# A decode kernel with a cached KV stream: loads alternate between K of the next job and V of the job in front of it

## The chip, the cores and the metric

The kernel runs on one core of one Trainium2 chip. The time is device microseconds (us). The kernel before took 631.83 us in the median of its first six runs (630.43 to 634.16). A profiled execution has a span (first to last instruction) a few microseconds shorter than the timed run; when a part of the span is quoted, it is from the profile.

## The reference, cut to what matters

The program runs two layers twice over a batch of eight single tokens: attention over a cached window, then an MLP, with the same weights and **the same caches** in both rounds.

```python
x = x + A(layernorm(x), k_cache, v_cache, wq, wo)   # round 0
x = x + B(layernorm(x), w1, b1, w2, b2)
x = x + A(layernorm(x), k_cache, v_cache, wq, wo)   # round 1, same caches
x = x + B(layernorm(x), w1, b1, w2, b2)
# A: W = 1024 cached positions, 32 heads of 128, 8 batch entries, bf16
#    p = softmax(q k^T / sqrt(128)); o = p v; out = o @ wo
# B: layernorm, w1, gelu, w2
```

K and V of one batch entry are 2 x 32 heads x 1024 x 128 in bf16. Each load brings two heads of K or V: a *unit* of 512 KB. The softmax is written without subtracting a maximum, so K of a group can be turned into scores as it comes.

## The kernel before

A *job* is one batch entry, one round, and eight head pairs (16 heads). A batch entry needs two jobs in round 0 and two in round 1. One of its two halves stays in SBUF between the rounds ("kept"); the other is loaded twice. So each batch entry costs 48 unit loads: 16 for each of two jobs of round 0 and 16 for the reloaded job of round 1. There are 24 unit buffers. A full kept half takes 16 of them, and 8 go round.

A small planner (class `Plan`) holds all tasks with their dependencies and assumed durations, plays them through in its own clock when the program is built, and emits the instructions of every engine in that order. On the chip each engine then runs its instructions strictly in order.

```python
NUNIT = 24                      # unit buffers of 512 KB
class Plan:
    HOP = 0.15
    LOAD_LATENCY = 1.9          # what the planner assumes for a load, plus 1.29 us of flow
    # ... emit(): an engine takes the ready task of lowest (rank, seq); loads go strictly in list order,
    #     each when the planner has a free "unit":
    #         landed = max(landed, now + self.LOAD_LATENCY) + t.flow; seen = landed + 0.4

def scores(job, z):             # z: group of four K units, 16 matmuls of N=512 on TensorE
    # ... needs all four K of the group, each transposed on VectorE first (turn)
    # afterwards the group's four buffers are free, unless the job is kept

def values(job, i):             # 16 matmuls per V unit; afterwards its buffer is free, unless kept

def add_loads(job):             # all K of a job, then all V
    job.loads = {}
    for which in "kv":
        for i in range(job.n):
            job.loads[which, i] = plan.add(SP, 0.07, lambda which=which, i=i: load(which, job, i),
                                           take="unit", flow=1.29)
            job.loads[which, i].pos = position[0]
            position[0] += 1

def chain(b, ...):              # batch entry b between the rounds, rank CHAIN = before everything else:
    # residual add, layernorm, w1, gelu, w2, layernorm, queries (160 matmuls), round_q, placed queries (qd2)
    # waits for the last job of round 0 of this entry

# order of the loads: l0[b] = the two jobs of round 0 (the second is kept), l1s[b] = the reloaded job of round 1
for job in l0[0]: add_loads(job)
# ... wo, w1, w2 (after load 32)
for job in l0[1]: add_loads(job)
for b in range(NB):
    if b < NB - 1: add_loads(l1s[b])
    if b + 2 < NB:
        for job in l0[b + 2]: add_loads(job)
add_loads(l1s[NB - 1])
```

The softmax here doesn't subtract the row's maximum and nothing guards it: scores larger than these inputs give would overflow.

## Time and profile before

| | |
|---|---|
| time, median of the first six runs | 631.83 us |
| span of the profiled run | 627.1 us |
| bytes moved, mean rate | 217.66 MB, 347 GB/s |
| steady period, residual add of one batch entry to the next (mean of six) | 70.4 us |
| the same if its 48 loads never stopped (48 x 1.28 us) | 61.5 us |

From the summary page of the kernel before: the span, the rate in 40 equal slices, and the packets.

```profile
span 627.1 us, 21695 instructions
...
GB/s 284 409 408 397 377 382 274 409 408 299 255 408 406 289 344 392 407 409 257 307 409 408 286 330 396 408 408 267 354 408 408 286 305 393 407 408 253 376 250 3
DMA packets 62720, 217.66 MB, mean 347 GB/s; under 512 B 6358, under 2 KB 12198, under 8 KB 61990
```

Undisturbed slices reach 406 to 409 GB/s. Between them lie slices at 255 to 299. The bytes alone take 217.66 MB / 409 GB/s = 532 us of the 627. The stream bounds the kernel, and what can be gained is in the slices where it falters.

One period from the timeline of VectorE (start, duration, line, operation, output<-inputs). The first and the third line are the residual adds that start the chains of two neighbouring entries; the second is the placement of the queries that ends the first chain.

```profile
...
279.74 0.13 DVE L531 TENSOR_TENSOR xT<-xT,att 128x5 f32<-128x5 f32 x1
...
301.39 0.81 DVE L351 TENSOR_TENSOR qd_151<-e_ps,mask_96 128x128 bf16<-128x128 f32 x4
...
351.65 0.12 DVE L531 TENSOR_TENSOR xT<-xT,att 128x5 f32<-128x5 f32 x1
```

The chain takes 301.39 - 279.74 = 21.7 us here, and the period 71.9 us. The windows of 3 us in that chain (columns: window, length, busy time and instruction count of each engine, granted clock, DMA share, GB/s):

```profile
...
core 0: us, PE busy (x) PEld busy (x) DVE busy (x) ACT busy (x) POOL busy (x), PEclk, DMA share, GB/s
...
282.00:285.00 3.00, 1.89 (x70) 1.89 (x70) 3.00 (x4) 0.00 (x0) 0.41 (x1) 0.50 0.71 281
285.00:288.00 3.00, 3.00 (x44) 1.12 (x42) 2.90 (x9) 0.22 (x1) 0.00 (x0) 0.50 0.04 12
288.00:291.00 3.00, 3.00 (x71) 1.76 (x68) 0.78 (x3) 0.00 (x0) 0.00 (x0) 0.50 0.73 217
...
300.00:303.00 3.00, 2.71 (x88) 2.71 (x88) 0.99 (x5) 0.18 (x1) 0.00 (x0) 0.50 0.18 60
303.00:306.00 3.00, 3.00 (x76) 1.97 (x77) 0.53 (x2) 0.00 (x0) 0.00 (x0) 0.50 0.90 304
```

The stream is dry twice, in 285-288 (12 GB/s) and in 300-303 (60 GB/s). The timeline of the queue that issues the loads (start, duration, instruction) tells why. Consecutive issues around the two holes:

```profile
...
276.06 0.54 SPq L364 DMA_DIRECT2D unit_124<-in_A_k_cache_dram  x1
287.51 0.54 SPq L364 DMA_DIRECT2D unit_118<-in_A_v_cache_dram  x1
...
293.29 0.54 SPq L364 DMA_DIRECT2D unit_124<-in_A_v_cache_dram  x1
301.72 0.54 SPq L364 DMA_DIRECT2D unit_118<-in_A_k_cache_dram  x1
```

From 276.06 to 287.51 nothing is issued: all eight circulating buffers hold K, and the first is freed only when four K have landed, been transposed and been scored. From 293.29 to 301.72 nothing is issued: eight V wait for their softmax and for the query matmuls. I call such gaps *issue holes*.

A measure used below: the *loss* of a stretch is its length minus its bytes / 409 GB/s. Over the second to the seventh chain of the kernel before the mean loss is 6.3 us inside the chain and 2.5 us between its end and the next chain.

### The profile page before, as it was taken

To read this page: it belongs to the slowest core of one execution; us is meant where nothing else is said; L and a number is where in the kernel's file an instruction comes from. 1 tells how busy PE (TensorE), PEld (TensorE's weight loads), DVE (VectorE), ACT (ScalarE), POOL (GpSimd) and SP (SyncE) were. 2 spreads that over 40 slices of the span, in tenths; PEclk is the share of its full clock that TensorE was granted. 3 is DMA by queue.
4 is the path that set the end of the run, shared out by engine and by line. 5 is a ranking of instruction groups with operands and counts; after the bars stand their busy time and mean duration, and the time that the engine had idled before them with its cause. 6 is when DMAs were issued, how large, how long until landed. Compare 5 with 4: busy or idle time off the path is not lost.

```text
span 627.1 us, 21695 instructions
## 1 busy us (share of the span) xinstructions
PE 438.7 (70%) x10016; PEld 307.6 (49%) x10016; DVE 308.0 (49%) x587; ACT 39.1 (6%) x115; POOL 13.9 (2%) x27
## 2 busy tenths in 40 slices
PE   1556319777777788668686788668777777668784
PEld 1333316555454564456363564456463564455474
DVE  2444044655536726645447726645546726545522
ACT  0000000000000001000000001000000001000000
POOL 2000000000000000000000000000000000000001
PEclk9999999999965556555655556555655556555655
DMA  7999997998799799997899799997999789997960
GB/s 284 409 408 397 377 382 274 409 408 299 255 408 406 289 344 392 407 409 257 307 409 408 286 330 396 408 408 267 354 408 408 286 305 393 407 408 253 376 250 3
DMA packets 62720, 217.66 MB, mean 347 GB/s; under 512 B 6358, under 2 KB 12198, under 8 KB 61990
## 3 DMA queue, kind: packets, MB, share of 16 engines
q1 hardware_dynamic: 62630, 216.29, 89.6%
q8 instruction: 78, 1.28, 0.8%
q14 instruction: 12, 0.10, 0.0%
HBM read 216.25 MB, written 0.01 MB: 345 GB/s over the span
## 4 chain that ended last, share of the span: by engine, by line
DMA 48%; PE 27%; issue 10%; DVE 8%; SPq 5%; POOL 0%; POOLq 0%; ACT 0%; DVEq 0%; ACTq 0%
DMA unit_127<-in_A_k_cache_dram 8%; DMA unit_119<-in_A_k_cache_dram 7%; PE s_ps L385 7%; PE o_ps L430 5%; PE q_ps L542 5%; DMA unit_118<-in_A_k_cache_dram 5%; DMA unit_119<-in_A_v_cache_dram 5%; DMA unit_127<-in_A_v_cache_dram 3%; PE o_ps L326 3%; PE h_ps L297 3%; DMA unit_137<-in_A_v_cache_dram 2%; DMA unit_131<-in_A_v_cache_dram 2%; DMA unit_135<-in_A_k_cache_dram 2%; DMA unit_136<-in_A_v_cache_dram 2%; DMA unit_133<-in_A_k_cache_dram 2%
## 5 line engine op out<-in xcount | busy, mean ns | idle before, releaser
L385 PEld LDWEIGHTS <-qd_150 128*16 128x16 bf16 x512 | 17.6, 103 | 82.7 <-issue 56.1
L454 PE MATMUL att<-ot,wo_sb 128*128 128x1 bf16 x1280 | 37.0, 165 | 24.2 <-DVE ot L445 12.2
L454 PEld LDWEIGHTS <-wo_sb 128*128 128x128 bf16 x1280 | 36.9, 104 | 25.4 <-issue 13.5
L542 PE MATMUL q_ps<-xn,wq_sb 128*128 128x1 bf16 x1280 | 35.8, 165 | 5.3 <-issue 5.3
L542 PEld LDWEIGHTS <-wq_sb 128*128 128x128 bf16 x1280 | 35.0, 104 | 7.3 <-issue 5.5
L297 PE MATMUL h_ps<-yT,w_sb 128*128 128x1 bf16 (+1 forms) x630 | 18.2, 166 | 28.8 <-DVE yT L265 26.0
L396 ACT ACTIVATE p_s<-s_ps 128x512 bf16<-128x512 f32 x32 | 19.1, 597 | 286.0 <-PE s_ps L385 286.0
L409 PE MATMUL sh_ps<-p_s,ident 128*32 128x64 bf16 x512 | 13.3, 238 | 33.6 <-DVE p_s L399 33.3
L399 DVE STREAM_TRANSPOSE p_s<-p_s 128x512 bf16<-128x512 bf16 x32 | 22.3, 697 | 26.8 <-ACT p_s L396 26.8
L422 DVE RECIPROCAL rd<-d_ps 128x16 f32<-128x16 f32 x32 | 7.9, 247 | 49.8 <-PE d_ps L418 49.8
L297 PEld LDWEIGHTS <-w_sb 128*128 128x128 bf16 x630 | 17.5, 104 | 29.6 <-DVE yT L265 15.7
L409 PEld LDWEIGHTS <-ident 128*32 128x32 bf16 x512 | 9.5, 117 | 41.9 <-DVE p_s L399 21.4
L385 PEld LDWEIGHTS <-qd_151 128*16 128x16 bf16 x512 | 13.8, 113 | 29.8 <-issue 26.6
L370 DVE STREAM_TRANSPOSE unit_118<-unit_118 128x1024 uint32<-128x1024 uint32 x12 | 14.9, 1242 | 23.4 <-DMA unit_118<-in_A_k_cache_dram 23.4
L260 POOL TENSOR_TENSOR ln_w<-ln_w,nhalf 128x1 f32<-128x1 f32 (+1 forms) x18 | 12.0, 665 | 602.2 <-DVE ln_w L257 598.1
L326 PEld LDWEIGHTS <-w_sb 128*128 128x128 bf16 x630 | 17.6, 104 | 12.0 <-issue 4.1
L351 DVE TENSOR_TENSOR qd_150<-e_ps,mask_96 128x128 bf16<-128x128 f32 x32 | 7.1, 282 | 29.7 <-PE e_ps L347 29.7
L370 DVE STREAM_TRANSPOSE unit_133<-unit_133 128x1024 uint32<-128x1024 uint32 x10 | 12.4, 1239 | 18.3 <-DMA unit_133<-in_A_k_cache_dram 18.3
L445 DVE TENSOR_TENSOR ot<-o_ps,rd 128x16 bf16<-128x16 f32 x16 | 2.5, 159 | 37.6 <-PE o_ps L430 37.6
L376 PE MATMUL s_ps<-ident,mask_l 2*128 2x512 bf16 x32 | 18.7, 586 | 0.0
L445 DVE TENSOR_TENSOR ot_149<-o_ps,rd 128x16 bf16<-128x16 f32 x16 | 3.6, 226 | 29.5 <-PE o_ps L430 29.5
L385 PE MATMUL s_ps<-unit_135,qd_150 128*16 128x512 bf16 x32 | 13.7, 566 | 5.8 <-DVE unit_135 L370 5.8
(304 smaller groups left out, 1158.3 us busy)
## 6 DMA issues: line engine op xcount, KB each, us to landing
unit_118<-in_A_k_cache_dram SPq DMA_DIRECT2D x12, 512.0 KB
unit_119<-in_A_k_cache_dram SPq DMA_DIRECT2D x12, 512.0 KB, 10.1
unit_120<-in_A_k_cache_dram SPq DMA_DIRECT2D x12, 512.0 KB
unit_121<-in_A_k_cache_dram SPq DMA_DIRECT2D x12, 512.0 KB, 15.1
unit_134<-in_A_k_cache_dram SPq DMA_DIRECT2D x11, 512.0 KB
unit_135<-in_A_k_cache_dram SPq DMA_DIRECT2D x11, 512.0 KB
unit_127<-in_A_k_cache_dram SPq DMA_DIRECT2D x11, 512.0 KB, 10.2
wq_sb<-in_A_wq_dram SPq DMA_DIRECT2D x5, 1024.0 KB, 6.8
```

The costliest lines, as they stand in the source:

```text
L260: nc.gpsimd.tensor_tensor(out=t["wv"][:], in0=t["wv"][:], in1=nhalf[:, 0:nb], op=ALU.pow)
L297: nc.tensor.matmul(t["h"][:, fc, :], lhsT=w1_sb[:, kc, fc * P:(fc + 1) * P], rhs=t["y"][:, kc, :], start=(kc == 0), stop=(kc == NKC - 1))
L326: nc.tensor.matmul(t["o"][:, n, :], lhsT=w2_sb[:, fc, n * P:(n + 1) * P], rhs=t["g"][:, fc, :], start=(fc == 0), stop=(fc == NFC - 1))
L370: nc.vector.transpose(t, t)
L376: nc.tensor.matmul(job.s_ps[:].rearrange("p (x u) -> p x u", u=2), lhsT=mask_l[:].rearrange("k x u i -> k (x u i)"), rhs=ident[0:2, None, ...
L385: nc.tensor.matmul(s_ps[32 * a:32 * a + 16, :].rearrange("p (t c) -> p t c", c=32), lhsT=qd[:, je, o:o + 16], rhs=k[:, je // 2, je % 2], s ...
L396: nc.scalar.activation(job.p_s[:], job.s_ps[:], ACT.Exp, scale=QSCALE, accum_out=job.rs[:])
L399: nc.vector.transpose(job.p_s[:], job.p_s[:])
L409: nc.tensor.matmul(job.sh_ps[32 * i:32 * i + 32, a], lhsT=ident[:, 32 * a:32 * a + 32], rhs=turned[:, :, 0:4, i], start=True, stop=True)
L430: nc.tensor.matmul(job.o_ps[:, 2 * i:2 * i + 2], lhsT=v[:, c * DH:(c + 1) * DH], rhs=job.p_v[:, a, c, 2 * z:2 * z + 2], start=(first and c ...
L454: nc.tensor.matmul(att[job.b][:, n:n + 1], lhsT=wo_sb[:, h, n * P:(n + 1) * P], rhs=job.ot[:, hi:hi + 1], start=(h == 0 and n == 0), stop= ...
L542: nc.tensor.matmul(t["q"][:, h:h + 1], lhsT=wq_sb[:, kc, h * DH:(h + 1) * DH], rhs=t["x"][:, kc, :], start=(kc == 0), stop=(kc == NKC - 1))
```

## The change

The intent: V of a job and K of the next job need different engines and different waiting. If they alternate, a V arrives when its probabilities have long been ready, so its buffer comes back at once; and VectorE, which needs 1.25 us for each K, sees a K only every 2.56 us.

```diff
+WP = (9, 16, 22, 26)
...
-    def add_loads(job):
-        job.loads = {}
-        for which in "kv":
-            for i in range(job.n):
-                job.loads[which, i] = plan.add(...)
+    def add_loads(jobs, extra):
+        for prev, job in zip([None] + jobs, jobs + [None]):
+            ks = [("k", job, i) for i in range(job.n)] if job else []
+            vs = [("v", prev, i) for i in range(prev.n)] if prev else []
+            while ks or vs:
+                for x in (ks, vs):
+                    if x:
+                        for f in extra.get(position[0], ()):
+                            f()
+                        add_load(*x.pop(0))
...
-    for job in l0[0]:
-        add_loads(job)
-    wo_ready = [...]
-    w_ready = [...]
-    # ... (the rest as shown above)
+    jobs = l0[0] + l0[1]
+    for b in range(NB):
+        jobs += [l1s[b]] + (l0[b + 2] if b + 2 < NB else [])
+    add_loads(jobs, {WP[0]: [first half of wo], WP[1]: [second half of wo], WP[2]: [w1], WP[3]: [w2]})
```

(The last lines are shortened: each entry of the dictionary adds one weight load ahead of the load with that number.)

Three things change at once: the *alternation*; a *shift*, since V of a job now comes with or after K of the next, so that the V that closes a batch entry lands eight loads later in the list; and the *weights*, which go in among the first 26 loads. The bytes, the 10016 matmuls and the 587 VectorE instructions stay.

More of the change, by code (lines that the diff above doesn't have):

```diff
@@ L48, in __init__ @@
         self.b, self.layer, self.p0, self.n, self.kept = b, layer, p0, n, kept
-        self.k, self.v = {}, {}
+        self.k, self.v, self.loads = {}, {}, {}
         self.o_ps = None
@@ L469, in _kernel, with add_load @@
     position = [0]
-    def add_loads(job):
-        job.loads = {}
-        for which in "kv":
-            for i in range(job.n):
-                job.loads[which, i] = plan.add(SP, 0.07, lambda which=which, i=i: load(which, job, i),
-                                               take="unit", flow=1.29)
-                job.loads[which, i].pos = position[0]
-                position[0] += 1
+    def add_load(which, job, i):
+        job.loads[which, i] = plan.add(SP, 0.07, lambda: load(which, job, i), take="unit", flow=1.29)
+        job.loads[which, i].pos = position[0]
+        position[0] += 1
+    def add_loads(jobs, extra):
[8 more added lines that the diff above has]
+                        add_load(*x.pop(0))
     def add_weights(us, fn):
@@ L588, in add_queries @@
         return expand(step, lambda: q1T[:, b, :], qd1)
-    for job in l0[0]:
-        add_loads(job)
-    wo_ready = [add_weights(7.0, lambda: load_wo(0, 16)), add_weights(7.0, lambda: load_wo(16, 32))]
-    w_ready = [add_weights(5.6, load_w1), add_weights(5.6, load_w2)]
-    for job in l0[1]:
-        add_loads(job)
-    for b in range(NB):
-        if b < NB - 1:
-            add_loads(l1s[b])
-        if b + 2 < NB:
-            for job in l0[b + 2]:
-                add_loads(job)
-    add_loads(l1s[NB - 1])
+    jobs = l0[0] + l0[1]
+    for b in range(NB):
+        jobs += [l1s[b]] + (l0[b + 2] if b + 2 < NB else [])
+    wo_ready, w_ready = [], []
+    add_loads(jobs, {
+        WP[0]: [lambda: wo_ready.append(add_weights(7.0, lambda: load_wo(0, 16)))],
+        WP[1]: [lambda: wo_ready.append(add_weights(7.0, lambda: load_wo(16, 32)))],
+        WP[2]: [lambda: w_ready.append(add_weights(5.6, load_w1))],
+        WP[3]: [lambda: w_ready.append(add_weights(5.6, load_w2))],
+    })
     qd = add_queries(0, [])
```

## The prediction

> **What bounds the kernel now.** The cache stream. The summary shows 217.66 MB at a mean of 347 GB/s, while undisturbed 3 us slices of the window table reach 401 to 416. (The Trainium skill, "DMA: Bandwidth & Descriptors", Specifications, gives a fabric ceiling of 435 GB/s; this trace never passes 416.) At 409 GB/s the bytes need 532 us of the 627 us span. A 512 KB unit lands every 1.28 us (issue spacing, 309-340 us). A steady period (one batch, 48 units) takes about 70 us against 48 x 1.28 = 61.5, so each of six loses about 8.5 us. At the end the stream stops at about 605 us and 21.6 us of work follow.
>
> **Where the loss sits.** While a batch's serial chain (layernorm, MLP, queries: 22.5 us from residual add to placed queries, 279.7 to 302.2) runs, 16 of 24 buffers hold kept K and V, so 8 circulate. The timeline of the DMA-issuing queue shows no issue from 276.1 to 287.5 (all eight hold K; scores wait for four landings, VectorE transposes of 1.25 us and 2.0 us of MLP matmuls) and none from 293.8 to 301.7 (eight V wait for softmax, 4.4 us of query matmuls and a 2.2 us pause). The window table shows 12 GB/s in 285-288 and 60 in 300-303.
>
> **What the change does.** No byte, matmul or vector instruction is added or removed; load order changes, every engine's order with it, and weights move into the first 26 loads. During a chain a V now arrives with its probabilities ready, so its buffer returns after about 0.5 us, and K arrives every 2.56 us, so transposes no longer crowd the chain. From the new instruction order I walk one steady chain by hand with the durations above. The first hole almost vanishes (estimate 0.5 us): four K are scored between the MLP products and five V are consumed before the queries. The second remains: the second K group is scored after the queries, leaving the queue empty for 3 to 5 us, plus a slow restart (a load issued into an empty queue at 301.7 landed 4.0 us later). Loss per period: about 5 us (estimate) for 8.5. Six periods gain about 21 us.
>
> **What it costs.** The V that closes a batch lands eight loads (10 us) later, so every chain starts later. That hurts at both ends: in the first chain the arriving K are kept, in the last they need queries not yet made; the eight buffers fill up and the stream should be nearly dry for 12 to 14 us in each (estimate), against about 6 us before. In the last chain part is offset: 24 loads follow its start, 32 before. Estimated starts: second chain 154 us (before 140), eighth 552 (before 562.7), then about 61 us to the end (before 64.5).
>
> **Predicted.** 615 us (-2.7%), range 602 to 629. Faster by over 2%: 0.60; within 2%: 0.34; slower: 0.06.
>
> **What would show it.** Issue holes of about 11 and 8 us per period become one of 6 to 8 us around the query matmuls; periods about 66 us; DMA share in 200-550 us up from 0.91-0.95 to about 0.96; a nearly dry stretch of over 10 us in the first chain (110-125 us) and in the last; PE and VectorE busy time unchanged within 2%.
>
> **What would make it wrong.** If K groups, now gathered over 10 us instead of 5, hold buffers so long that the stream stalls outside the chain, the gain vanishes. If V values queue behind the chain on PE, holes stay at 8 us. If the first and last chains overlap better than my walk says, it is below 602.

## The result and the profile after

| | before | after |
|---|---|---|
| median | 631.53 us (20 runs) | 651.36 us (10 runs) |
| ratio, 95% interval | | 1.031, 1.0285 to 1.0334 |
| span | 627.1 us | 649.1 us |
| second chain starts (1) | 140.3 us | 157.4 us |
| mean of the six periods from there | 70.4 us | 71.8 us |
| eighth chain starts | 562.7 us | 588.3 us |
| from there to the end | 64.4 us | 60.8 us |
| mean chain, second to seventh | 21.0 us | 25.6 us |

(1) Read from the residual adds on VectorE, as in the timeline above.

A ratio is the mean time of one kernel's fast runs over that of the other's of the same rounds, so it is not quite the ratio of the medians.

The change made the kernel 3.1% slower. The 22 us of span are: 17.1 before the second chain, 8.5 in the six periods, and -3.6 at the end. The shift moves eight loads (8 x 1.28 = 10.2 us) from behind the last chain to in front of the second, so as time lost the account reads: 6.9 us before the second chain, 8.5 in the periods, 6.6 at the end.

The same lines of the summary page, after:

```profile
span 649.1 us, 21675 instructions
...
GB/s 288 398 388 400 378 408 316 166 391 375 321 306 407 398 306 285 404 408 350 308 313 407 376 326 311 409 407 320 277 385 406 363 341 238 410 408 316 150 246 3
DMA packets 62720, 217.66 MB, mean 335 GB/s; under 512 B 6358, under 2 KB 12198, under 8 KB 61990
```

The bytes and the packets are the same to the digit. The mean rate is 335 GB/s instead of 347; low slices (166, 150) stand near both ends. The third chain on VectorE, with the start of the next. The second and the third line make the inputs of the first MLP matmuls (yT) and of the query matmuls (xn):

```profile
...
229.25 0.17 DVE L539 TENSOR_TENSOR xT<-xT,att 128x5 f32<-128x5 f32 x1 [0.59 <-PE att L455]
...
232.79 0.24 DVE L266 TENSOR_SCALAR yT<-xT,ln_mv,ln_w 128x5 bf16<-128x5 f32 x1
...
245.44 0.25 DVE L266 TENSOR_SCALAR xn<-xT,ln_mv,ln_w 128x5 bf16<-128x5 f32 x1
...
254.90 0.85 DVE L352 TENSOR_TENSOR qd_151<-e_ps,mask_96 128x128 bf16<-128x128 f32 x4
...
300.55 0.17 DVE L539 TENSOR_TENSOR xT<-xT,att 128x5 f32<-128x5 f32 x1 [0.59 <-PE att L455]
```

This chain takes 254.90 - 229.25 = 25.7 us, where the one shown of before took 21.7. Windows of 3 us in it (columns as before):

```profile
...
228.00:231.00 3.00, 3.00 (x76) 2.89 (x74) 2.18 (x6) 0.37 (x1) 0.00 (x0) 0.50 0.91 300
231.00:234.00 3.00, 0.95 (x36) 0.87 (x34) 1.96 (x7) 0.00 (x0) 0.54 (x1) 0.50 0.96 285
...
237.00:240.00 3.00, 2.65 (x55) 1.40 (x48) 1.50 (x4) 0.22 (x1) 0.00 (x0) 0.50 0.70 264
240.00:243.00 3.00, 2.87 (x79) 2.78 (x77) 1.47 (x3) 0.00 (x0) 0.00 (x0) 0.50 1.04 333
...
246.00:249.00 3.00, 2.42 (x90) 2.42 (x91) 1.17 (x1) 0.00 (x0) 0.00 (x0) 0.50 1.03 419
...
252.00:255.00 3.00, 2.55 (x33) 0.93 (x25) 1.27 (x2) 0.69 (x2) 0.00 (x0) 0.50 0.21 38
255.00:258.00 3.00, 2.79 (x44) 1.20 (x48) 1.61 (x7) 0.37 (x1) 0.00 (x0) 0.50 0.94 317
```

There is no window as dry as 285-288 was, but there are more low ones: of the fourteen windows from 222 to 264 us, one stands at 38 GB/s and eight at 264 to 333 (not all shown). Note 231-234: the DMA engines are busy for 0.96 of the window and move 285 GB/s. By the issues and the landings that the trace tells, about four or five loads are under way there. The same number are under way in 246-249, at 419 GB/s, so the number alone does not explain the low rate; the low windows lie in a hole or just behind one. The queue that issues:

```profile
...
219.96 0.55 SPq L365 DMA_DIRECT2D unit_134<-in_A_v_cache_dram  x1
227.01 0.54 SPq L365 DMA_DIRECT2D unit_128<-in_A_k_cache_dram  x1
...
234.45 0.53 SPq L365 DMA_DIRECT2D unit_125<-in_A_k_cache_dram  x1
238.66 0.54 SPq L365 DMA_DIRECT2D unit_130<-in_A_v_cache_dram  x1
...
243.44 0.54 SPq L365 DMA_DIRECT2D unit_130<-in_A_v_cache_dram  x1
247.20 0.54 SPq L365 DMA_DIRECT2D unit_128<-in_A_k_cache_dram  x1
253.27 0.54 SPq L365 DMA_DIRECT2D unit_136<-in_A_v_cache_dram  x1
```

The two holes have become four: 7.0 us before the chain starts, then 4.2 (234.45 to 238.66), 3.8 (243.44 to 247.20) and 6.1 us (247.20 to 253.27). They add up to 21 us, where the two holes before added up to 17 us in three of five chains (20 in the one shown). Now the chain of waits through this stretch (start, length, what; each piece was released by the one above it):

```profile
...
214.20 10.35 DMA unit_126<-in_A_v_cache_dram
...
224.59 0.59 PE o_ps L431 x16
225.18 1.92 PE s_ps L386 x12
227.10 0.45 SPq L365
...
227.65 6.13 DMA unit_125<-in_A_v_cache_dram
...
233.83 0.59 PE o_ps L431 x16
234.42 1.87 PE h_ps L298 x70
...
239.93 6.61 DMA unit_128<-in_A_v_cache_dram
```

A V that lands at 224.54 (issued at 214.20, one of the last behind a deep queue) is followed on TensorE by the second score group of the *next* job, and only that group, at 227.1, frees buffers. The reason lies in the load list: the V that alternate with these K belong to the half that is kept, so that using them frees nothing; the eight circulating buffers hold the four K of that group and four later loads that cannot be used before it. Its last K, issued at 212.22, landed at 223.26. The V issued at 227.65, after the hole, needs 6.13 us to land. TensorE waits for it, and the first MLP matmuls stand behind it. The same happens again from 239.93 to 246.58, in front of the query matmuls. TensorE's own records of these two waits (last bracket: idle time and what ended it):

```profile
...
233.83 0.59 PE L431 MATMUL o_ps<-p_v,unit_125 128*128 128x2 bf16 x16 [2.04 <-DMA unit_125<-in_A_v_cache_dram]
...
246.58 0.59 PE L431 MATMUL o_ps<-p_v,unit_128 128*128 128x2 bf16 x16 [3.17 <-DMA unit_128<-in_A_v_cache_dram]
...
253.19 0.29 PE L348 MATMUL e_ps<-qT,sel 128*128 128x32 bf16 x4
```

TensorE is idle for 5.2 us here. Not all of it is lost to the chain: yT was ready at 233.03 and xn at 245.69, so the matmuls behind the two V started about 1.3 us late each. The last line shows a third delay without any idle time: e_ps, which spreads the finished queries, stood behind a score group of four K and started 1.5 us after its input (qT, ready at 251.66). This delay of 1.5 us occurs in each of the six chains; the waits for V come to 3.8 us a chain in TensorE's idle time and to about 1.5 us in delay of the two matmul groups (means of the second to seventh chain). The chain grew by 4.6 us in the mean. The kernel before has no wait for V inside a chain.

The first chain is the other place. Its windows after:

```profile
...
111.00:114.00 3.00, 2.24 (x85) 2.27 (x85) 1.02 (x3) 0.00 (x0) 0.00 (x0) 1.00 0.19 74
...
120.00:123.00 3.00, 3.00 (x102) 2.70 (x99) 1.50 (x3) 0.19 (x1) 0.00 (x0) 1.00 0.02 5
123.00:126.00 3.00, 2.06 (x17) 0.47 (x16) 0.63 (x4) 0.00 (x0) 0.00 (x0) 1.00 0.56 175
```

From 111 to 126 us the rate is 5 to 212 GB/s. Here the K that arrive are kept K, which free nothing, so the eight circulating buffers fill up.

### The profile page after: what moved, and what is told of

It reads as the page before. It is cut to its first block, busy times and chain, and to the rows that moved or that the text cites. A ratio compares the mean times of both kernels' runs of the same rounds, so it can differ in the third digit from the quotient of the medians.

```text
span 649.1 us, 21675 instructions
## 1 busy us (share of the span) xinstructions
PE 421.8 (65%) x10016; PEld 305.1 (47%) x10016; DVE 313.9 (48%) x587; ACT 39.1 (6%) x115; POOL 14.0 (2%) x27
## 3 DMA queue, kind: packets, MB, share of 16 engines
q8 instruction: 78, 1.28, 0.8%
## 4 chain that ended last, share of the span: by engine, by line
DMA 71%; PE 16%; issue 7%; SPq 3%; DVE 2%; POOL 0%; POOLq 0%; ACT 0%; DVEq 0%
PE s_ps L386 6%; DMA unit_141<-in_A_v_cache_dram 5%; DMA unit_125<-in_A_v_cache_dram 4%; DMA unit_127<-in_A_v_cache_dram 4%; PE q_ps L550 3%; DMA unit_139<-in_A_v_cache_dram 3%; DMA unit_124<-in_A_v_cache_dram 3%; DMA unit_134<-in_A_v_cache_dram 3%; DMA unit_140<-in_A_v_cache_dram 3%; DMA unit_126<-in_A_v_cache_dram 3%; DMA unit_120<-in_A_v_cache_dram 3%; DMA unit_118<-in_A_v_cache_dram 3%; DMA unit_138<-in_A_v_cache_dram 3%; DMA unit_128<-in_A_v_cache_dram 3%; DMA unit_132<-in_A_v_cache_dram 3%
## 5 line engine op out<-in xcount | busy, mean ns | idle before, releaser
L386 PEld LDWEIGHTS <-qd_150 128*16 128x16 bf16 x512 | 13.7, 108 | 37.6 <-issue 36.9
L386 PEld LDWEIGHTS <-qd_151 128*16 128x16 bf16 x512 | 13.6, 111 | 26.6 <-issue 18.2
L371 DVE STREAM_TRANSPOSE unit_130<-unit_130 128x1024 uint32<-128x1024 uint32 x15 | 18.7, 1246 | 9.3 <-DMA unit_130<-in_A_k_cache_dram 9.3
L377 PE MATMUL s_ps<-ident,mask_l 2*128 2x512 bf16 x32 | 19.3, 604 | 0.0
L371 DVE STREAM_TRANSPOSE unit_120<-unit_120 128x1024 uint32<-128x1024 uint32 x9 | 11.2, 1241 | 15.7 <-DMA unit_120<-in_A_k_cache_dram 15.7
L371 DVE STREAM_TRANSPOSE unit_118<-unit_118 128x1024 uint32<-128x1024 uint32 x10 | 12.4, 1244 | 12.9 <-DMA unit_118<-in_A_k_cache_dram 12.9
L386 PE MATMUL s_ps<-unit_118,qd_150 128*16 128x512 bf16 x36 | 17.2, 617 | 1.9 <-DVE unit_118 L371 1.6
L415 ACT CAST p_v<-sh_ps 128x256 bf16<-128x256 f32 x32 | 11.9, 373 | 105.0 <-PE sh_ps L410 105.0
L431 PE MATMUL o_ps<-p_v,unit_141 128*128 128x2 bf16 x192 | 7.1, 166 | 16.6 <-DMA unit_141<-in_A_v_cache_dram 15.4
L371 DVE STREAM_TRANSPOSE unit_129<-unit_129 128x1024 uint32<-128x1024 uint32 x8 | 9.9, 1238 | 16.4 <-DMA unit_129<-in_A_k_cache_dram 16.4
L371 DVE STREAM_TRANSPOSE unit_140<-unit_140 128x1024 uint32<-128x1024 uint32 x8 | 10.0, 1245 | 16.2 <-DMA unit_140<-in_A_k_cache_dram 16.2
L386 PE MATMUL s_ps<-unit_130,qd_151 128*16 128x512 bf16 x36 | 16.9, 620 | 0.0
```

Source lines behind the costliest of these rows:

```text
L371: nc.vector.transpose(t, t)
L377: nc.tensor.matmul(job.s_ps[:].rearrange("p (x u) -> p x u", u=2), lhsT=mask_l[:].rearrange("k x u i -> k (x u i)"), rhs=ident[0:2, None, ...
L386: nc.tensor.matmul(s_ps[32 * a:32 * a + 16, :].rearrange("p (t c) -> p t c", c=32), lhsT=qd[:, je, o:o + 16], rhs=k[:, je // 2, je % 2], s ...
L415: nc.scalar.copy(job.p_v[:], job.sh_ps[:])
L431: nc.tensor.matmul(job.o_ps[:, 2 * i:2 * i + 2], lhsT=v[:, c * DH:(c + 1) * DH], rhs=job.p_v[:, a, c, 2 * z:2 * z + 2], start=(first and c ...
```

## The experiments

Theories:

- **ORDER**: TensorE runs in a fixed order, planned with a load latency of 1.9 us; V stand ahead of the chain's matmuls and have not landed.
- **GATHER**: a group of four K now takes eight loads to come together and holds buffers all the while.
- **SHIFT**, later made precise as **ENDS**: what costs is that the closing V and the chain come eight loads later, and that this is paid in the first and the last chain.
- **BUFFERS**: with eight circulating buffers, no order of loads can keep the queue filled through a chain.

Medians and ratios are against the kernel before in the same rounds (3 rounds each; its medians were 630.2 to 631.3 us). The granted clock differs between executions but does not follow the time: executions of the changed kernel at 0.66 and at 0.93 took 650.0 and 651.9 us. "Period" is the mean from the second chain's start; where the shift is taken back before the end, the shortened last period is left out.

| run | median us | ratio | second chain starts | period us | last chain to end |
|---|---|---|---|---|---|
| after_blk8 | 646.27 | 1.0236 | 162.5 | 69.3 | 64.3 |
| after_blk4 | 651.91 | 1.0331 | 159.4 | 71.5 | 62.5 |
| after_lat4 | 642.10 | 1.0169 | 156.4 | 70.4 | 59.1 |
| after_lat6 | 641.70 | 1.0178 | 155.9 | 71.2 | 57.2 |
| after_wp32 | 648.51 | 1.0281 | 157.2 | 70.8 | 61.4 |
| after_lastfix | 640.51 | 1.0165 | 157.7 | 71.0 | 64.7 |
| before_wpearly | 633.64 | 1.0050 | 144.2 | 70.4 | 64.8 |
| before_lat4 | 630.68 | 0.9984 | 139.8 | 70.7 | 65.6 |
| mid_blk1 | 634.43 | 1.0054 | 149.4 | 71.2 | 65.0 |
| mid_blk1_lat4 | 629.68 | 0.9986 | 149.4 | 70.4 | 64.6 |
| mid_blk8 | 625.95 | 0.9902 | 150.1 | 70.2 | 65.6 |
| mid_blk8_lat4 | 623.65 | 0.9883 | 150.1 | 69.9 | 64.2 |
| before_half24 | 635.93 | 1.0087 | 146.2 | 71.0 | 65.4 |
| before_half26 | 619.40 | 0.9812 | 146.1 | 68.2 | 62.6 |
| after_half26 | 619.88 | 0.9827 | 160.8 | 66.6 | 56.7 |
| mid_blk1_lat4_half26 | 607.03 | 0.9620 | 152.8 | 66.5 | 62.3 |

All are correct except the four "half" runs, which are wrong.

### after_blk8: the shift without the alternation

```diff
                 for x in (ks, vs):
-                    if x:
+                    for _ in range(min(8, len(x))):
```

> The changed kernel, but the loads go in blocks: eight K of the next job, then eight V of the job in front (the shift and the early weights stay, the alternation goes). Theory GATHER (a group of four K now takes eight loads to come together and holds buffers meanwhile): the steady period goes back to 70.4 us or less and only the later start remains, so about 641 us. Theory SHIFT (what costs is that the closing V and with it the chain come eight loads later; alternation is neutral): stays at 651 +- 3 us with periods near 71.8. Theory ORDER (PE runs values in a fixed order inside the chain and waits for V that have not landed): the chain, 25.3 us in the changed kernel, shortens to about 20-22 us because no V stands between the chain's first matmuls, about 640-645 us.

Measured: 646.27 us; periods 69.3 us, chains 22.5 us, second chain at 162.5 us. Without the alternation the periods are 1.1 us *shorter* than before, and all of the loss, more than all of it, lies at the ends. So the shift in itself does not lengthen a period. It does cost at the ends: 162.5 - 140.3 - 10.2 = 12.0 us before the second chain, and 64.3 - 64.4 + 10.2 = 10.1 us at the end.

### after_blk4: the same in fours

```diff
-                    if x:
+                    for _ in range(min(4, len(x))):
```

> The changed kernel with blocks of four K, four V. GATHER: a K group gathers in four loads, as in the kernel before, so nearly all of the loss per period comes back: periods 70.4 us or less, about 640 us. SHIFT: 651 +- 3 us. ORDER: V still stand inside the chain, in fours; chain 23-25 us, 645-651 us.

Measured: 651.91 us, periods 71.5 us. Here a K group gathers in four loads, just as before, and nothing comes back. GATHER, as the cause of the longer period by itself, is refuted. (The chains were 21.9 us, shorter than I expected under ORDER, and the period did not follow. So the length of the chain is not the whole story either.)

### after_lat4 and after_lat6: a planner that expects loads later

```diff
-    LOAD_LATENCY = 1.9
+    LOAD_LATENCY = 4.0      # 6.0 in after_lat6
```

> The changed kernel; only the planner's assumed latency of a load goes from 1.9 to 4.0 us (the trace shows 4 to 6.6 us from issue to landing after a hole), so it places fewer values ahead of the chain's matmuls. ORDER: waits of PE for V inside the chain (2.0 and 3.2 us in the third chain) go, the chain shortens from 25.3 to about 21 us, periods to 69 or less, total about 635 us. GATHER and SHIFT: the chain may shorten, but the period does not follow; 648-652 us.

> Dose: planner's latency 6.0 us. ORDER: waits for V inside the chains (3.8 us a chain in the changed kernel, 1.5 us at 4.0) fall to under 1 us, chain about 20 us, total as at 4.0 or slightly less: 638-643 us. If the gain at 4.0 was an accident of one order: anywhere, for instance back at 650.

Measured: 642.10 and 641.70 us, both about 9 us better than the change as it was. The waits of TensorE for V inside the chains (mean of the second to seventh) went from 3.8 us to 1.5 us at 4.0 and to nothing at 6.0, and the chains from 25.6 to 21.0 and 19.6 us. The third chain of after_lat6 on VectorE:

```profile
...
226.62 0.17 DVE L539 TENSOR_TENSOR xT<-xT,att 128x5 f32<-128x5 f32 x1 [0.59 <-PE att L455]
...
245.45 0.88 DVE L352 TENSOR_TENSOR qd<-e_ps,mask 128x128 bf16<-128x128 f32 x4 [3.94 <-PE e_ps L348]
...
```

It takes 18.8 us, where the changed kernel took 25.7. ORDER is right about the waits. What is worth 9 us is the edit, and the edit plans TensorE's whole order anew: at 6.0 the score group ahead of e_ps is gone too (e_ps starts within 0.1 us of its input in all six chains). So the runs show that the fixed order cost 9 us, not that the waits for V alone did. ORDER is wrong about the size: I had expected 635, and at 6.0, with no wait left, there is no further gain. The periods are 70.4 and 71.2 us, no shorter than in the kernel before.

### before_lat4: the control for it

```diff
-    LOAD_LATENCY = 1.9
+    LOAD_LATENCY = 4.0      # in the kernel before
```

> Control: the kernel before with the planner's latency at 4.0 us instead of 1.9. If the 9 us that the same edit brought to the changed kernel came from V standing ahead of the chain (ORDER), little happens here, where no V stands inside the chain: 628-634 us. If the planner's latency was simply wrong for any order, this gains some 9 us too: about 622 us.

Measured: 630.68 us, ratio 0.9984 with an interval from 0.9954 to 1.0014. The old order has no V inside the chain and gains nothing from the edit. The 9 us belong to the new order of loads.

### before_wpearly and after_wp32: the weights alone

In the kernel before, the weights go to loads 9, 16, 22 and 26 and the order of K and V stays; in the changed kernel, they go back behind load 32.

```diff
-        WP[0]: [...], WP[1]: [...], WP[2]: [...], WP[3]: [...],
+        32: [all four],
```

> The kernel before with one part of the change alone: the weights at loads 9, 16, 22 and 26 instead of after load 32. All theories: the same bytes precede the second chain, so within 1% of the kernel before (625-638 us); if the early weights were the cause of the 17 us by which the second chain starts later, this would be about 640 us or more.

> The changed kernel with the weights after load 32, as before, instead of inside the first 26 loads. Alone, early weights cost the kernel before 0.5%; here the first part up to the second chain (157.4 us) may shorten by about 3 us: 646-651 us. If early weights were chosen because alternation needs them, it gets slower: over 655 us.

Measured: 633.64 us (ratio 1.0050, interval 1.0024 to 1.0075) and 648.51 us (from 651.36). Early weights cost about 3 us in the kernel before. In the changed kernel the medians differ by as much, but the four runs with late weights spread from 644.96 to 651.55 us, so that there it is not clear of noise. They are not what delays the second chain: it starts at 157.2 us with late weights.

### mid_blk1, after_lastfix, mid_blk1_lat4: the ends

The list of jobs is cut into parts, and K and V alternate only inside a part. In the mid runs the first two jobs and the last two stand alone (K then V, as before), with the weights after load 32. In after_lastfix only the last two do.

```diff
-    add_loads(jobs, {...})
+    for part in (jobs[:1], jobs[1:2], jobs[2:-2], jobs[-2:-1], jobs[-1:]):   # lastfix: jobs[:-2], jobs[-2:-1], jobs[-1:]
+        add_loads(part, {...})
```

> The changed kernel with alternation load by load, but the shift begins only after the first chain's batch and is taken back before the last chain (the first two and last two jobs load all K, then all V), weights after load 32. Theory ENDS (13.5 us of the 22 us lost lie before the second and after the eighth chain, because a shifted first and last chain has only kept or unusable K to load): span falls by 10 to 14 us, to about 637-641 us timed, with periods still near 71.8. Rival: the shift's cost is paid once wherever it happens: 648-652 us.

> The changed kernel with the shift taken back before the last chain only (the last two jobs load all K, then all V); the start is untouched. ENDS says that about half of its loss is there (10.2 us of structure less the 3.6 us the changed kernel's last part is shorter): 651.4 - 6.6 = about 645 us (642-647). If all lay in the first chain: 650 or more.

> Alternation load by load, ends not shifted, planner's latency 4.0 us. If the losses of ends and of order add up (17 us and 9 us of the changed kernel's 651), this is 634.4 less about 8: 626 us (623-629). If they overlap: 630 or more.

Measured: mid_blk1 634.43 us, 16.9 us less than the change as it was, even a little more than I expected; its periods stay at 71.2 us and its chains at 25.6 us. So most of the 20 us lost lay at the ends: 10.9 us with the last chain alone repaired (after_lastfix, 640.51 us; in the profiles 8.4 us of it lie behind the start of the seventh chain), and the rest at the first, with about three of that for the weights. With the planner's latency as well (mid_blk1_lat4) the kernel is at 629.68 us, ratio 0.9986. The two repairs do not quite add up (I expected 626). What they leave is the kernel before, to within the interval (0.9956 to 1.0015). **With ends and order repaired, alternation as such neither costs nor gains anything, though I had predicted 3.5 us per period for it.**

### mid_blk8 and mid_blk8_lat4: a version that beats both

Parts as above, and blocks of eight instead of single loads; the second with the planner's latency at 4.0.

> The same with blocks of eight. Periods were 69.3 us in the run with blocks of eight, 1.1 us less than before. ENDS: the ends cost nothing more than before, so 6 x 1.1 = 7 us are gained: about 624 us (621-628). Rival, shift paid once anywhere: about 634 us or more.

> The same with blocks of eight and the planner's latency at 4.0 us. Its chains were 22.4 us long against 20.2 before, so if ORDER holds for blocks too, they shorten to about 20 and periods to about 68.5: 617-624 us; otherwise as the run without it.

Measured: 625.95 us (0.9902) and 623.65 us (0.9883, interval 0.9841 to 0.9926). Both are correct, and both are faster than either kernel, by 1.0 and 1.2%. The planner's part was smaller than I expected, and the intervals of the two overlap. That mid_blk8 came near its 624 us is in part luck: the periods of 69.3 us that were to bring the gain did not come (70.2 us). In the profile of mid_blk8_lat4 5.6 us are gained, of which 3.8 lie behind the start of the seventh chain (the eight shifted loads allowed for) and 1.4 in the five periods before it. (The chains of 22.4 and 20.2 us in the last expectation are means of the third to the seventh.)

### Four runs with other buffers

The question left open: why does the period not shorten? To get room for two more load buffers I made the second MLP weight keep 7 of its 14 row blocks. Both halves are loaded, into the same place, so the bytes stay and the result is wrong.

```diff
-    w2_sb = wpool.tile([P, NFC, D], BF16, name="w2_sb")
+    w2_sb = wpool.tile([P, 7, D], BF16, name="w2_sb")
-                    nc.tensor.matmul(t["o"][:, n, :], lhsT=w2_sb[:, fc, n * P:(n + 1) * P],
+                    nc.tensor.matmul(t["o"][:, n, :], lhsT=w2_sb[:, fc % 7, n * P:(n + 1) * P],
-NUNIT = 24
+NUNIT = 26              # 24 in the control
```

> Control for the next three, wrong on purpose: the second MLP weight keeps 7 of its 14 row blocks in SBUF (both halves are still loaded, into the same place), which frees 8.75 KB per partition that is not used here. Same loads and matmuls as the kernel before: 629-634 us.

> Wrong on purpose as the control; the freed space holds two more load buffers, so 10 instead of 8 circulate beside the 16 kept. BUFFERS (what bounds a chain is the number of circulating buffers, whatever the load order): each of the two issue holes per chain (11.4 and 5.9 us) shortens by up to 2.6 us, periods from 70.4 to 66-68, total 607-620 us. If buffers do not bind: within 1% of the control.

> The changed kernel, wrong on purpose as the control, with 26 buffers. BUFFERS: its holes (7.5, 4.2, 3.8 and 6.1 us) shorten too, periods from 71.8 to 66-68, ends gain some as well: 620-632 us. If what failed in my estimate is only the order of values on PE, not buffers: over 642 us.

> Alternation with its ends not shifted, planner's latency 4.0 us, 26 buffers, wrong on purpose. With 24 it equals the kernel before (629.7 for 630.2). If alternation needs more buffers to pay (a K group now holds four of them over eight loads), it is now 1% or more below the 26-buffer kernel in the old order; if alternation has no merit of its own, it equals it within 1%.

Measured: the control is at 635.93 us, 0.9% above the kernel before and just out of my range; its delay lies before the second chain (146.2 us), and its periods are 71.0 us (the profile is of its slowest execution, 639.74 us). Two more buffers bring the old order to 619.40 us (periods 68.2), the change as it was to 619.88 us (periods 66.6 instead of 71.8), and the alternation with repaired ends to 607.03 us (periods 66.5). So two buffers are worth about 2.8 us per period in the old order and 5.2 us in the changed one (there against the changed kernel itself; a control with the small weight and 24 buffers was not run in the changed order). The issue holes of the third chain in after_half26:

```profile
...
220.31 0.54 SPq L365 DMA_DIRECT2D unit<-in_A_v_cache_dram  x1
225.26 0.54 SPq L365 DMA_DIRECT2D unit<-in_A_k_cache_dram  x1
...
231.13 0.54 SPq L365 DMA_DIRECT2D unit<-in_A_k_cache_dram  x1
235.74 0.54 SPq L365 DMA_DIRECT2D unit<-in_A_v_cache_dram  x1
...
241.32 0.54 SPq L365 DMA_DIRECT2D unit<-in_A_k_cache_dram  x1
248.50 0.54 SPq L365 DMA_DIRECT2D unit<-in_A_v_cache_dram  x1
```

They are 5.0, 4.6 and 7.2 us long, three instead of four, and the first comes with a deeper queue ahead of it: the seven loads before it went out at 1.28 us intervals. In mid_blk1_lat4_half26 the loss inside a chain falls to 2.1 us (mean of five chains), against 5.1 us in before_half26 and 6.3 us in the kernel before. TensorE's waits for V are down to 1.4 us a chain without any edit of the planner.

This answers the question in part. With eight circulating buffers the alternation has no merit; with ten, and with its ends and order repaired, the new order is 2.0% faster (607.03 for 619.40) than the old order with ten; unrepaired it only breaks even there (619.88). It needs more buffers than it was given. Two things were not run with ten: blocks of eight, so that it is not shown whether the 2% belong to the alternation or to the shift; and the old order with the planner's latency at 4.0 (with eight it gained nothing).

## Why the prediction was wrong, point by point

- **Bound by the stream; the two holes and their causes: right.** The bytes are the same, and the time follows the rate.
- **Costs at the ends: right.** I predicted a stream "nearly dry for 12 to 14 us in each". The losses from 111 to 132 us and from 588 to 621 us add up to about 12 and 14 us. I predicted 61 us from the eighth chain to the end, and it is 60.8; the second chain at 154 us, and it is 157.4. That the 61 fits so well is in part luck: TensorE waits 5.8 us for V in that chain, which the walk did not have, and after_lat6, without these waits, needs 57.2 us.
- **The step that failed: "Loss per period: about 5 us (estimate) for 8.5."** It is 71.8 - 61.5 = 10.3 us. Instead of gaining 21 us, the six periods lost 8.5. There are three parts to this error.
  - *The comparison was uneven.* My 5 us came from a walk through the chain alone; the 8.5 us were of the whole period. Of the latter 2.5 us lie between chains, and they stayed (3.3 us after).
  - *"The first hole almost vanishes (estimate 0.5 us)".* It did not. It moved ahead of the chain (7.0 us in the chain shown, 6.0 to 7.5 in the second to seventh), where my walk did not look: I had counted on V whose buffers return after 0.5 us, but the eight V just ahead of a chain are kept and return none, and in the chain shown everything waits for the second group of K. It is the stall outside the chain that I had named as a risk; gathering K in four loads (after_blk4) did not remove it, though. And I had counted a restart once and at 4.0 us. The change issues again behind each of its holes, with loads landing 6.1 and 6.6 us after issue in the chain shown, at 285 to 333 GB/s. With ten circulating buffers the period of the changed kernel is 66.6 us, the 66 that I predicted for eight. That is a coincidence and does not make the walk right for ten: after_half26 has three holes (5.0, 4.6 and 7.2 us) where the walk has one, and gains 1.6 us per period on the old order with ten (68.2), where I predicted about 4 on the old order with eight.
  - *"five V are consumed before the queries".* They are (seven in the chain shown), but TensorE waits for them: 3.8 us a chain. I had named V queueing behind the chain as a risk; the reverse happened, the chain queued behind V, and its last step behind a score group. The runs with a later planner remove the waits, at 6.0 the score group too, and 9 us with them.
- **"transposes no longer crowd the chain": right and worth little.** Without waits for V (after_lat6) the chain is 18.8 us at its shortest, where it was 19.3 before.
- **Signs I named.** Holes: four instead of one. DMA share in 200-550 us: 0.92, not 0.96 (before 0.93), and 351 GB/s for 359. PE busy fell by 3.9% and VectorE's rose by 1.9%, with the same instructions, so "unchanged within 2%" missed for PE.

The loss of the measured change is therefore made up of the ends (16.9 us with the weights, mid_blk1), and the fixed order on TensorE (9 us, after_lat4). They overlap: together they give 21.7 us. What was missing against the prediction is the gain per period; two more buffers bring a part of it (1.6 to 1.7 us per period on the old order with as many), not all.

What stays open: why blocks of eight in the middle gain 1% with 24 buffers where single loads gain nothing (most of it behind the start of the seventh chain, as said above), how much of the 2% with ten buffers is the alternation, why the rate is low just after a hole, and the pauses of 1 to 2 us in TensorE's query matmuls that the profile puts to no releaser; they occur in some chains of every kernel and move single periods by about 2 us.

## What to carry to other kernels

When loads wait for buffers, ask for every order how many buffers go round at the tightest moment, and test a new order with two more of them before judging it: here the repaired alternation is worth nothing with eight and 2% with ten. When the instruction order of an engine is planned ahead, look up in the trace how long loads take to land just after a hole, since that is where the engine waited for them here: 4.0 us in place of 1.9 in the planner was worth 9 us in the new order and nothing in the old one. A software pipeline shifted by one stage paid at both ends here (16.9 us with the weights); if the first and the last stage are special (kept data, data not yet usable), leave them unshifted.

## What the Trainium skill lacked or had wrong

- "DMA: Bandwidth & Descriptors", section "Anatomy of one DMA", gives a fit of 2.0 us plus bytes / 436 GB/s for one DMA on the software path, which makes 3.2 us for 512 KB (an estimate from that fit). For the hardware path, which this kernel uses, I found no time from issue to landing there, only a first-byte latency of about 0.6 us. The runs show 4.0 us for a unit issued when one load was left in the queue (301.7 us, before; that load landed at 302.45) and 6.1 and 6.6 us for units issued second or third after a hole (227.65 and 239.93 us, after), with about two or three loads still ahead of them.
- The same page has no figure for the rate just after a hole in the issues. Here windows of 3 us there (228-234, 240-246 and 255-261, after) moved 285 to 333 GB/s while the DMA engines showed shares of 0.91 to 1.04, so a full share of busy time is not full rate; undisturbed windows moved 401 to 419 GB/s. Its fabric ceiling of 435 GB/s (Specifications) agrees with the highest window seen, 429 GB/s.
- "Trainium Kernel Development and Optimization", Best Practices, says that consistent bubbles can mean that SBUF or PSUM ran out. The runs agree, and give a size: two more buffers of 4 KB per partition, beside eight in circulation, were worth about 2.8 us of a 71.0 us period in one order and 5.2 of 71.8 in the other.
- "TensorE: Matmul & The Clock Gate", section "Seeing it yourself", warns that trace events of the clock gate are not always reliable. No run here shows a wrong event, but a gap that misleads in the same way: the profile of the kernel before gives a granted clock of 1.00 at 96.4-98.3 us, though its first clock record comes only at 172.3 us. The score matmuls there took 0.59 to 0.63 us, as they did at a recorded 0.50; at a recorded 1.00 (258.2 us, after) they took 0.39 to 0.40.
